# A recurrent attention block and a mixture of experts in one program: the low part of each split weight tile on GpSimd instead of VectorE

## Chip, cores and metric

The kernel runs on one core of a Trainium2 chip. The metric is the device time of one execution in microseconds; three runs of the kernel before gave 1008.19, 1009.38 and 1009.79 us, so the median is 1009.38 us. Engine names are those of the profile: PE is TensorE's matrix multiplication and PEld its weight load, DVE is VectorE, ACT is ScalarE, POOL is GpSimd, SP is SyncE, which here only issues DMAs.

## The reference

A gated linear attention, step by step in time, gives `x`; a mixture of four small two-layer networks is then applied to `x` and summed with normalised weights.

```python
for t in range(S):                      # B, H, S, D = 4, 8, 768, 48
    state = alpha[:, :, t, :, None] * state + einsum('bhd,bhe->bhde', k[:, :, t], v[:, :, t])
    y[:, :, t] = einsum('bhd,bhde->bhe', q[:, :, t], state)
x = y.transpose(0, 2, 1, 3).reshape(B * S, H * D)          # 3072 x 384
p = domain_probs / (domain_probs.sum(-1, keepdims=True) + 1e-09)
for e in range(E):                      # 4 experts, w1 384 x 1024, w2 1024 x 384
    out += p[:, e:e + 1] * (np.maximum(x @ w1[e], 0.0) @ w2[e])
```

## The kernel before

The sequence is cut into 24 units of 128 time steps (six chunks, four batches), and each unit's attention is a Python generator (`attention`, L422) that yields after every beat. Inside a unit a loop over seven levels doubles the block length. At each level ACT copies a part of the queries (L487), DVE multiplies the queries by decays (L494), shortens the decays (L496), ACT copies keys (L505), DVE multiplies the keys (L506), PE forms products (L513), and DVE puts them under a mask (L523). L539, L464 and L453 are other DVE multiplications, L434 the transposes that bring the inputs into place. So ACT and DVE take turns through a unit.

The units are gathered in groups: the first of two units, the others of four. For each group and expert, `up` (L660) multiplies by `w1` and `down` (L723) by `w2`. Group 0 works with plain fp32 weights and activations (L689, L764 with `raw`). From group 1 on both operands are split in two fp32r parts, a rounded top part and the remainder, and three products replace one (`PRODUCTS`, L95; L695 and L764 with `w`). The remainder of the hidden layer is made by L720 on DVE, for which PE can wait.

The weight tiles are split once, while group 0 and group 1 are computed. A piece is a quarter of one expert's `w1` or `w2`, 128 x 768 elements; there are 16 of each, 32 in all. `load_piece` (L178) brings the whole piece into a `raw` buffer (12 of them) by a DMA of SP. `split_piece` (L200) is a generator in two steps: the first takes a `w` buffer (four for each layer) and lets ACT write the rounded part `top` (L208); the second, one call of `background` (L213) later, subtracts it from the whole (L210) and stores both parts to HBM as one DMA of 768 KB from POOL's queue (L211). Later groups load both parts back from there (L185). In group 1 the pieces of `w2` are also used directly from the buffer in which they were made, by L764 in `down`.

The order of the instructions on each engine is the order in which the Python code calls them: the schedule is written out by hand. `background` is called after each step of `up`, and at some steps of `down`; `making` holds pieces not yet begun and `splitting` those with their second step to come. `advance` (L858) brings in the beats of attention by due times that the code computes from fixed costs. Each engine works through its own list in order, and waits on semaphores where it needs another's result.

Apart from the split, POOL has memsets in the first 10 us, and 22 stores of results (L799). For two of these units (the first group's) the store is issued between the stores of the 18th and 19th pieces.

Of the kernel before, what the change touches and what calls it, by code (L numbers as in the profile page):

```python
# [10 lines left out]
F32 = mybir.dt.float32  # L11
# [9 lines left out]
def kernel(  # L21
# [11 lines left out]
    nc = tc.nc  # L33
# [138 lines left out]
    def parts_of(l):  # L172
        return wts.tile([P, 2, KC * QF], F32R, name=f"w{l + 1}", bufs=AHEAD if l == 0 else NQ)
# [26 lines left out]
    def split_piece(l, i):  # L200
        gi, k = divmod(i, E * NQ)
        whole = wt[l][i]
        w = parts_of(l)
        if l == 1:
            wt[l][i] = w
        top, rest = (w[:, part] for part in range(2))

        nc.scalar.copy(out=top, in_=whole)  # L208
        yield
        nc.vector.tensor_sub(rest, whole, top.bitcast(F32))  # L210
        nc.gpsimd.dma_start(out=kept[l][k], in_=w.bitcast(F32))  # L211

    def background():  # L213
# [446 lines left out]
    def up(gi, e, fc, slots=None):  # L660
# [12 lines left out]
        if fresh(gi) and fc in beside:  # L673
            making.append(split_piece(1, first_piece(gi, e) + beside[fc]))
        if gi == 0 and e > 0 and fc in SPLIT_AT:
            making.append(split_piece(0, e * NQ + SPLIT_AT[fc]))
# [46 lines left out]
    def down(gi, e, slots):  # L723
# [4 lines left out]
        if gi == 0 and e < E - 1 and slots[0] == (e == 0):  # L728
            making.extend(split_piece(0, first + NQ + k) for k in range(2))
# [134 lines left out]
    with tc.manual_schedule():  # L864
# [46 lines left out]
        for gi, e in tasks:  # L911
            rest = gi == e == 0
# [37 lines left out]
```

## Time and profile before

| | |
|---|---|
| runs, us | 1008.19, 1009.38, 1009.79 |
| profiled execution, us | 1008.34 |
| its span, us | 1006.6 |
| granted TensorE clock, mean | 0.998 |
| L208, ACT, 128x768, 32 times | 26.4 us, 828 ns each, 37.5 to 288.7 us |
| L210, DVE, 128x768, 32 times | 30.3 us, 951 ns each, 38.8 to 293.9 us |
| L211, POOL, issue of a store, 32 times | 17.2 us, 537 ns each; 7.8 us to landing (median) |
| DVE, all | 569.3 us |
| POOL, all | 36.0 us |

The span is the time from the first to the last instruction of the program on the core; the device time has 1.7 us around it. Mean durations are of one instruction. The chain of waits is followed back from the last instruction, at each step to what released it or to the instruction in front of it on its engine; an instruction that isn't on it ended early enough. An engine's busy time includes time in which an instruction is held up after it has begun.

### The profile page before, as it was taken

The numbers are of one execution on the slowest core, as the hardware profiler recorded it, in microseconds if no ns is written. First come the engines' busy times: TensorE is split into PE (matmuls) and PEld (weight loads), VectorE is DVE, ScalarE is ACT, GpSimd is POOL, SyncE is SP. The second block draws the span as 40 slices with busy tenths as digits, with TensorE's granted clock in tenths as the row PEclk, the third lists the DMA queues.
The fourth block names the chain that finished last, engine by engine and source line by source line (L and its number), as shares of the span: only waits on it lengthen the run. The fifth ranks groups of instructions, "written<-read, shape, count | busy, mean of one in ns | idle before, by whom it ended". The sixth has DMA issues, their size and how long they took to land.

```text
span 1006.6 us, 20815 instructions
## 1 busy us (share of the span) xinstructions
PE 986.5 (98%) x8468; PEld 877.8 (87%) x8468; DVE 569.3 (57%) x1202; ACT 422.2 (42%) x928; POOL 36.0 (4%) x79
## 2 busy tenths in 40 slices
PE   8899899999999999999999999999999999999998
PEld 7767678988989889889899899898898989999998
DVE  5788878477666555566646635756576521222222
ACT  4677656454463542532543514445443422111111
POOL 2000001000000000000000000000000000000000
PEclk9999999999999999999999999999999999999999
DMA  9898989595776593764955928757757405151511
GB/s 190 264 295 214 308 267 346 165 336 142 284 256 203 195 272 96 263 216 136 312 166 160 305 99 236 246 134 277 225 156 251 158 2 202 49 210 41 199 68 32
DMA packets 160623, 200.81 MB, mean 199 GB/s; under 512 B 88432, under 2 KB 136944, under 8 KB 160528
## 3 DMA queue, kind: packets, MB, share of 16 engines
q1 hardware_dynamic: 154064, 169.66, 54.6%
q0 software_dynamic: 6016, 29.49, 7.5%
q8 instruction: 67, 1.10, 0.5%
q10 hardware_dynamic: 448, 0.33, 0.1%
q14 instruction: 28, 0.23, 0.1%
HBM read 169.56 MB, written 29.88 MB: 198 GB/s over the span
## 4 chain that ended last, share of the span: by engine, by line
PE 86%; DVE 7%; ACT 3%; issue 2%; DMA 1%; SPq 0%; DVEq 0%; POOL 0%; ACTq 0%; POOLq 0%
PE ops L764 38%; PE one L695 34%; PE sc L513 5%; PE yps L608 3%; ACT qb L487 1%; PE sps L639 1%; DVE w L210 1%; DVE near L523 1%; PE tp L236 1%; PE far L569 1%; PE one L689 1%; DVE QT L494 1%; DVE QT L434 1%; DVE hT L720 1%; DVE KT L506 1%
## 5 line engine op out<-in xcount | busy, mean ns | idle before, releaser
L764 PE MATMUL ops<-w,hT 128*128 128x384 f32 x2112 | 381.1, 338 | 0.6 <-DVE hT L720 0.6
L764 PEld LDWEIGHTS ops<-w,hT 128*128 128x128 f32 x2112 | 364.3, 188 | 5.2 <-DVE hT L720 1.8
L695 PE MATMUL one<-xT,w 128*128 128x512 f32 x1440 | 338.3, 393 | 0.0
L695 PEld LDWEIGHTS one<-xT,w 128*128 128x128 f32 x1440 | 268.8, 188 | 57.5 <-DVE hT L720 0.2
L697 ACT ACTIVATE hT<-one 128x512 fp32r<-128x512 f32 (+1 forms) x192 | 107.9, 562 | 295.3 <-PE one L695 294.3
L720 DVE SCALAR_TENSOR_TENSOR hT<-one,hT 128x512 fp32r<-128x512 f32 (+1 forms) x192 | 121.7, 642 | 116.0 <-ACT hT L697 116.0
L487 ACT COPY qb<-QT 64x256 f32<-64x256 f32 x322 | 131.3, 408 | 85.7 <-DVE QT L494 42.7
L494 DVE TENSOR_TENSOR QT<-QT,AT 128x256 f32<-128x256 f32 x158 | 66.7, 422 | 89.1 <-ACT qb L487 88.4
L790 DVE SCALAR_TENSOR_TENSOR acc<-ops,p_all,acc 128x384 f32<-128x384 f32 x66 | 38.2, 612 | 92.3 <-PE ops L764 92.2
L523 DVE COPY_PREDICATED near<-masks,sc 128x256 f32<-128x256 uint8 x138 | 73.9, 536 | 16.3 <-PE sc L513 13.7
L513 PEld LDWEIGHTS sc<-qb,KT 128*64 128x64 f32 x2208 | 69.8, 138 | 9.2 <-issue 4.4
L513 PE MATMUL sc<-qb,KT 128*64 128x64 f32 x2208 | 74.3, 223 | 3.1 <-ACT qb L487 3.0
L506 DVE TENSOR_TENSOR KT<-KT,AT 128x256 f32<-128x256 f32 x161 | 67.3, 418 | 0.8 <-PE tp L236 0.8
L505 ACT COPY KT<-KT 128x256 f32<-128x256 f32 x138 | 57.6, 418 | 3.3
L689 PE MATMUL one<-xT,raw 128*128 128x256 f32 (+1 forms) x240 | 45.1, 340 | 0.4 <-ACT xT L406 0.4
L764 PE MATMUL ops<-raw,hT 128*128 128x384 f32 x128 | 44.7, 492 | 0.0
L689 PEld LDWEIGHTS one<-xT,raw 128*128 128x128 f32 x240 | 38.1, 191 | 5.2 <-ACT xT L406 0.6
L445 ACT ACTIVATE AT<-AT,ident 128x512 f32<-128x512 f32 x22 | 15.9, 724 | 63.5 <-DVE AT L434 62.6
L496 DVE TENSOR_TENSOR AT<-AT 128x256 f32<-128x256 f32 (+1 forms) x138 | 39.2, 284 | 4.7
L799 POOL DMA_DIRECT2D out_dram<-acc x22 | 11.8, 540 | 680.2 <-DVE acc L790 680.2
L608 PE MATMUL yps<-lat,rv 128*32 128x128 f32 x736 | 33.1, 273 | 2.6 <-ACT lat L586 2.6
L764 PEld LDWEIGHTS ops<-raw,hT 128*128 128x128 f32 x128 | 23.2, 190 | 13.7 <-issue 0.6
(110 smaller groups left out, 638.5 us busy)
## 6 DMA issues: line engine op xcount, KB each, us to landing
w<-kept SPq DMA_DIRECT2D x144, 768.0 KB, 6.9
kept<-w POOLq DMA_DIRECT2D x32, 768.0 KB, 7.8
raw<-in_moe_w_dram SPq DMA_DIRECT2D x48, 384.0 KB, 7.5
rv<-in_v_dram SPq DMA_DIRECT2D x24, 192.0 KB, 2.9
rk<-in_k_dram SPq DMA_DIRECT2D x22, 192.0 KB, 3.6
rq<-in_q_dram SPq DMA_DIRECT2D x22, 192.0 KB, 7.8
out_dram<-acc POOLq DMA_DIRECT2D x22, 192.0 KB, 2.3
sa<-in_alpha_dram SPq DMA_DIRECT2D x44, 88.0 KB, 2.6
```

Source lines behind the costliest of these rows:

```text
L487: nc.scalar.copy(out=qb[rows, :, i, :].rearrange("p a (b r) -> p a b r", r=m), in_=qv[rows])
L494: nc.vector.tensor_mul(qv, qv, spread(dv[:, :, :, 0], m))
L505: nc.scalar.copy(out=new[:, :, :, 1, :], in_=old[:, :, :, 1, :])
L506: nc.vector.tensor_mul(new[:, :, :, 0, :], old[:, :, :, 0, :], spread(halved(decs[li])[:, :, :, 1], m))
L513: nc.tensor.matmul(out[HALF * s:HALF * (s + 1), 2 * p:2 * p + 2, :], lhsT=KTs[li][:, p, HALF * s:HALF * (s + 1)], rhs=qbs[li][:, p, :, QUA ...
L523: nc.vector.copy_predicated(near.rearrange("p a (b two r) -> p a b two r", two=2, r=m)[:, :, :, 1, :], mk.unsqueeze(1).broadcast_to([P, H, ...
L608: nc.tensor.matmul(yps[QUAD * j:QUAD * (j + 1), c, :], lhsT=lhsT, rhs=rhs, start=begins, stop=ends)
L689: nc.tensor.matmul(one, lhsT=w[:, kc], rhs=xTs[gi][:, 0, kc, lo:hi], start=(kc == 0), stop=(kc == KC - 1))
L695: nc.tensor.matmul(one, lhsT=w[:, of_w, kc], rhs=x_part(gi, of_x)[:, kc, :n], start=k == 0, stop=k == len(turns) - 1)
L697: nc.scalar.activation(out=parts[0], in_=one, func=ACT.Relu)
L720: nc.vector.scalar_tensor_tensor(out=low, in0=x, scalar=0.0, in1=top.bitcast(F32), op0=ALU.max, op1=ALU.subtract)
L764: nc.tensor.matmul(sums[slot], lhsT=h, rhs=w, start=(n == begins[slot]), stop=(n == ends[slot]))
```

## The change

```diff
         nc.scalar.copy(out=top, in_=whole)
         yield
-        nc.vector.tensor_sub(rest, whole, top.bitcast(F32))
+        nc.gpsimd.tensor_sub(rest, whole, top.bitcast(F32))
         nc.gpsimd.dma_start(out=kept[l][k], in_=w.bitcast(F32))
```

All 32 subtractions leave DVE's list and stand on POOL's list, each directly in front of its own store. The order of what is left on DVE, and of everything on PE, ACT and SP, stays as it was. In front of the first subtraction the build puts one instruction on POOL that fetches the code for it. The store waits for a semaphore of its own engine now, and POOL's subtraction carries the waits for `top`, for the loaded piece and for the buffer that DVE's carried.

## The prediction

> **What bounds the kernel now.** First the page's busy line and its slices, to see which engine sets the pace and where the work on the split lies.
>
> ```profile
> span 1006.6 us, 20815 instructions
> PE 986.5 (98%) x8468; PEld 877.8 (87%) x8468; DVE 569.3 (57%) x1202; ACT 422.2 (42%) x928; POOL 36.0 (4%) x79
> PE   8899899999999999999999999999999999999998
> DVE  5788878477666555566646635756576521222222
> ```
>
> A slice is 25.2 us. PE is at 9 nearly everywhere; below it are only the first two slices, the fifth and the last, and in the first six DVE is at 5 to 8. So I cut the span into stretches and read PE's busy time of each:
>
> ```profile
> 25.00:50.00 25.00, 21.87 (x249) 18.01 (x248) 18.15 (x41) 17.38 (x44) 2.27 (x4) 1.00 0.80 263
> 50.00:75.00 25.00, 23.18 (x182) 17.16 (x180) 21.74 (x44) 17.63 (x43) 2.12 (x4) 1.00 0.95 293
> 75.00:100.00 25.00, 23.13 (x282) 18.23 (x284) 20.75 (x46) 17.89 (x41) 1.60 (x3) 1.00 0.83 213
> 100.00:125.00 25.00, 21.95 (x246) 15.90 (x241) 22.48 (x49) 16.16 (x38) 1.59 (x3) 1.00 1.00 312
> 125.00:150.00 25.00, 23.71 (x188) 18.29 (x187) 17.67 (x40) 14.62 (x34) 1.06 (x2) 1.00 0.85 262
> ...
> 200.00:225.00 25.00, 24.43 (x186) 21.44 (x188) 18.87 (x35) 13.99 (x29) 2.13 (x4) 1.00 0.96 316
> ```
>
> The columns after the length are busy us of PE, PEld, DVE, ACT and POOL. From 25 to 150 us PE is idle for 3.13 + 1.82 + 1.87 + 3.05 + 1.29 = 11.2 us, and DVE is the fullest of the feeding engines (22.48 of 25). From 150 to 350 us PE lacks 0.7 us in all (0.57 of it in the line of 200 to 225). The change touches work between 37 and 295 us, so it can win only what PE stands idle up to 225, and above all before 150.
>
> Next the line that moves, and then the chain of waits (start, length, what):
>
> ```profile
> L210 DVE TENSOR_TENSOR w<-raw,w x32: 944/949/977, 38.8 to 293.9; 128x768 fp32r<-128x768 f32 x32
> ...
> 58.06 0.83 ACT w L208
> 58.92 0.96 DVE w L210
> 59.88 0.34 DVE QT L494
> ```
>
> L210 takes 0.95 us each time. Of the 32, 16 run before 150 us: four at 38 to 44, where DVE has gaps, and twelve from 57 to 137, where it has next to none. On the chain up to 150 us stand six of these (58.92, 62.13, 68.54, 83.02, 88.06, 132.21), together 5.67 us. After 150 seven more stand on it, but beside a PE that is full.
>
> **The change part by part.** Removed from DVE: 32 x 0.95 = 30.3 us. The four early ones run in gaps and are worth nothing. The last 16 are covered by PE's queue of L695 and L764; what they can give is the 0.57 us that PE waited at 214 us for L720. The twelve between are 12 x 0.95 = 11.4 us, with 5.67 on the chain: half. I use that share for DVE time that comes and goes in this stretch.
>
> Added to POOL: 32 subtractions of 128x768. No row has such an operation. The nearest are POOL's memsets, which only write.
>
> ```profile
> L873 POOL MEMSET rv<- 128x640 f32 x2 | 1.2, 629 | 0.1
> L875 POOL MEMSET st<- 128x384 f32 x3 | 1.2, 439 | 0.0
> ```
>
> They give 0.742 ns an element ((629 - 439)/256), so one pass over 768 is 629 + 128 x 0.742 = 724 ns, the lower bound. Two reads and a write, one after the other, add two passes of 570 ns: 1.86 us, the upper bound. I take 1.87 us, since the operation has three streams. The Trainium skill (GPSIMD Engine Reference, "Elementwise — side-by-side cycle accounting") gives 4497 ns for 2048 elements with two inputs, by proportion an estimate of 1.69 us; by it the sum below would be about 0.7 us better, and no run shown here has it.
>
> POOL's length is itself hidden. POOL is 4% busy, and per piece it now holds 1.87 us and the store's issue of 0.54 (L211). L208's end leads L210's start by up to 7 us (3 in the mean) because DVE is serving other work, so most subtractions end earlier than they do now, and with them the store, the load's reuse of `raw`, and PE's first use of `rest` in group 1 (down starts at 172.5 and 212.9 us; on POOL the four subtractions before them end near 164 and 210, now at 166 and 212). Behind a subtraction in POOL's queue stand only its own store, the next piece, and two L799 stores (0.54 each at 155.5 us, data ready), so nobody new waits for POOL. The first one also needs POOL's code for it, which the changed program fetches in an instruction of its own; POOL's 30 us of idle time before 40 us cover that. Without that cover it would delay the first store, which is not read back before 137.9 us.
>
> What remains is whether the two engines disturb each other while reading the same memory. No row shows POOL computing on inputs beside DVE. One end: not at all, nothing is lost. Other end: a DVE instruction with two inputs in SBUF (L494, L496, L506, L539, L464, L453) waits until POOL's subtraction is done. That I count on the timeline: POOL starts 0.08 us after L208 ends (my allowance; L210 follows it by 0.03 us where it had only that to wait for), holds 1.87 us, and the loss is what is left of it when the first such DVE instruction is due, L210 taken out. One example:
>
> ```profile
> 78.53 0.83 ACT L208 CAST w<-raw 128x768 fp32r<-128x768 f32 x1
> ...
> 79.77 0.56 DVE L621 TENSOR_TENSOR xT<-yps,xT 128x384 fp32r<-128x384 f32 x1 [1.32 <-ACT xT L620]
> 80.24 0.41 DVE L494 TENSOR_TENSOR QT<-QT,AT 128x256 f32<-128x256 f32 x1
> ```
>
> L208 ends at 79.36, POOL holds 79.44 to 81.31, L621 reads PSUM and passes, L494 is due at 80.25: 1.06 us lost. For the twelve pieces, in order: 1.2, 0, 1.15, 0.2, 1.05, 0 to 1.4, 0.5, 0, 0.45, 0.6 to 1.35, 1.2, 1.05: together 7.4 to 9.6 us, 0.6 to 0.8 each. I take this end rather than none, because instructions on two inputs fill about half of DVE's time here and POOL starts exactly where they come thickest; the other end is the first rival. The Trainium skill (SBUF — State Buffer, "Who interferes with whom") says that such a VectorE instruction and a GpSimd instruction that reads SBUF exclude each other for a whole instruction; no run shown here bears it out or refutes it, and it would leave the count as it stands.
>
> Sum: (11.4 - 8.5) x 0.5 = 1.4 us gained, between 0.9 and 2.0. Against the profiled run (1008.34 us, span 1006.6 and 1.7 around it): 1006.9. That run lies 1.0 us below the median shown, so on the median's scale 1009.4 - 1.4 = 1008.0.
>
> **The rivals.**
> *DVE is not held up at all.* For it: ACT reads SBUF beside DVE all the time, and L494 keeps 0.42 us. Against: L487 reads one tile, and no row has a second engine reading two. The 5.67 us leave the chain, but L487 on ACT, whose copies alternate with L494 level by level and stand on the chain with 8% from 25 to 165 us, takes over part: between half and all of 5.67, with 0.6 at 214 us at best. Middle 4.2: 1005.2; at best 1003.1.
> *The wait costs more than the instruction did* (the other side). Place: the level loop from 50 to 137 us, where L494 follows ACT's copies directly. ACT's next instruction after L208 is often the very copy that L494 waits for, and without L210 in front of it L494 is due earlier, just after POOL has begun. My count uses starts from a DVE that was not yet rearranged. It decides from 0.95 us of loss per piece on (11.4/12). With 1.5 us it is (18 - 11.4) x 0.5 = 3.3 us slower, 1012.7; with the full 1.87 each time (22.4 - 11.4) x 0.5 = 5.5, 1014.9. For it: up to seven of the twelve counted losses already lie at 1.05 or more. Against: the transposes L434 (1.1 us) and L523, which do not read two tiles of SBUF, give POOL cover.
> *Something else takes the wait.* The chain has DMA waits in the same stretch (2.38 us at 54.78 for `sq`, 2.01 at 95.97) that would just begin earlier: 1009.4.
>
> **How the numbers follow.** Under 0.2% (2 us) a measurement of this kernel can't tell from no change. My forecast has 0.38: split by its spread into faster 0.14, same 0.16, slower 0.08. No hold-up 0.20: faster 0.19, same 0.01. Costlier wait 0.35: slower 0.33, same 0.02. Other wait 0.07: same 0.05, 0.01 to each side. Sum: faster 0.34, same 0.24, slower 0.42. The forecast's own range is 1006.5 to 1009.5; with the rivals' ends it is 1003.2 to 1015.0.
>
> **What would show it.** Right: 32 POOL tensor operations of about 1.9 us; L494, L496, L506 or L464 lengthened (or started late) by 0.5 to 1.9 us beside them and of the old length elsewhere; DVE's busy sum in 50 to 150 us little changed; PE's idle time before 150 us near 10 us; from 150 us on everything shifted by one amount. Wrong: those DVE lines at their old 0.42 us beside POOL (first rival), PE idle over 13 us before 150 (second), new waits of PE for `w` from POOL, or of ACT's L208 for a late store, or a POOL operation beyond 2 us.

## The result, and the profile after

The changed kernel takes 1013.78 us (median of six runs, 1013.24 to 1014.93) beside 1009.09 us of the kernel before: a ratio of 1.0046, 95% interval 1.0030 to 1.0061. It is slower by 4.7 us, where the forecast had it 1.4 us faster. The profiled execution has 1014.51 us and a span of 1012.3, 5.7 more than before. First the page's busy line:

```profile
span 1012.3 us, 20818 instructions
PE 987.2 (98%) x8468; PEld 877.6 (87%) x8468; DVE 566.6 (56%) x1170; ACT 422.5 (42%) x928; POOL 96.5 (10%) x111
```

32 instructions have left DVE, each of 0.95 us, 30.3 us in all. But DVE's busy time fell only from 569.3 to 566.6 us. Nearly all of the other 27.6 us must be in instructions that were there before (about three of them are L210's overlap with its neighbours). The groups by line show which, first of the kernel before, then of the changed one:

```profile
L506 DVE TENSOR_TENSOR KT<-KT,AT 128x256 f32<-128x256 f32 x161 | 67.3, 418 | 0.8 <-PE tp L236 0.8
L494 DVE TENSOR_TENSOR QT<-QT,AT 128x256 f32<-128x256 f32 x158 | 66.7, 422 | 89.1 <-ACT qb L487 88.4
...
L453 DVE TENSOR_TENSOR rk<-rq,rk 128x384 f32<-128x384 f32 x22 | 12.0, 545 | 0.0
```

```profile
L494 DVE TENSOR_TENSOR QT<-QT,AT 128x256 f32<-128x256 f32 x158 | 78.4, 496 | 92.8 <-ACT qb L487 91.9
L523 DVE COPY_PREDICATED near<-masks,sc 128x256 f32<-128x256 uint8 x138 | 74.0, 537 | 16.2 <-PE sc L513 13.7
L506 DVE TENSOR_TENSOR KT<-KT,AT 128x256 f32<-128x256 f32 x161 | 72.5, 450 | 0.9 <-PE tp L236 0.9
...
L453 DVE TENSOR_TENSOR rk<-rq,rk 128x384 f32<-128x384 f32 x22 | 16.1, 733 | 0.6 <-DMA rq<-in_q_dram 0.6
```

L494 went from a mean of 422 to 496 ns, L506 from 418 to 450, L453 from 545 to 733. L523, which reads a mask and PSUM, stayed (536, now 537). The timeline shows single ones; first DVE, then POOL, in the place that the prediction worked through:

```profile
80.44 0.56 DVE L621 TENSOR_TENSOR xT<-yps,xT 128x384 fp32r<-128x384 f32 x1 [1.31 <-ACT xT L620]
80.91 1.33 DVE L494 TENSOR_TENSOR QT<-QT,AT 128x256 f32<-128x256 f32 x1
...
82.40 2.56 DVE L506 TENSOR_TENSOR KT<-KT,AT 128x256 f32<-128x256 f32 x1
...
80.12 1.84 POOL L210 TENSOR_TENSOR w<-raw,w 128x768 fp32r<-128x768 f32 x1 [10.11 <-ACT w L208]
82.26 0.57 POOL L211 DMA_DIRECT2D kept<-w  x1 [0.30 <-DMA sq<-in_q_dram]
82.85 1.82 POOL L210 TENSOR_TENSOR w<-raw,w 128x768 fp32r<-128x768 f32 x1
```

L621 (one operand in PSUM) runs its usual 0.56 us beside POOL. L494, usually 0.42, stays until 82.24, just past the end of POOL's subtraction at 81.96. L506 stays from 82.40 to 84.96, past the end of the next one at 84.67. Over the span 20 instructions are lengthened, all of L494, L506, L453, L539 and L464, by 24.3 us together and by at most 2.13 us.

The stretches show what it cost (busy us of PE, PEld, DVE, ACT, POOL after the length):

```profile
25.00:50.00 25.00, 21.85 (x249) 18.01 (x248) 16.10 (x37) 17.47 (x44) 9.72 (x8) 1.00 0.76 235
50.00:75.00 25.00, 22.90 (x182) 17.38 (x180) 20.80 (x39) 16.89 (x42) 9.64 (x8) 1.00 0.99 316
75.00:100.00 25.00, 21.36 (x214) 16.22 (x216) 21.09 (x40) 16.59 (x37) 7.22 (x6) 1.00 0.85 225
100.00:125.00 25.00, 21.94 (x288) 16.23 (x284) 20.20 (x46) 17.73 (x42) 7.34 (x6) 1.00 1.01 310
125.00:150.00 25.00, 23.56 (x217) 18.53 (x208) 16.88 (x35) 13.94 (x32) 4.79 (x4) 1.00 0.74 233
150.00:175.00 25.00, 24.27 (x167) 18.46 (x167) 20.05 (x33) 13.51 (x27) 10.83 (x10) 1.00 1.06 350
...
200.00:225.00 25.00, 23.92 (x149) 20.49 (x148) 19.11 (x32) 16.67 (x34) 9.72 (x8) 1.00 0.83 253
...
250.00:275.00 25.00, 24.20 (x259) 21.70 (x259) 19.11 (x37) 13.00 (x29) 5.44 (x5) 1.00 1.02 344
```

PE idles 13.4 us from 25 to 150 us (before: 11.2), and it now idles in three stretches after that, 2.6 us in these lines, where it had been full but for 0.6. Laid beside those of before, DVE's instructions run 2.4 us late at 147 us and 5.5 us late from 304 us on. So the loss comes in both stretches, and ends where the last subtraction ends (297 us).

Before 150 us the hold reaches PE by way of ACT. PE's products of line 569 wait for a copy of ACT. From 50 to 150 us these waits (total, times, longest) were, in the kernel before:

```profile
PE far L569 <- ACT qb L487: 2.2, 2, 1.3
```

and in the changed one:

```profile
PE far L569 <- ACT qb L487: 5.1, 3, 1.9
```

DVE is held, ACT's copy L487 starts late, and PE waits for that copy. All of PE's waits there together grow from 7.9 to 10.2 us.

### The profile page after: what moved, and what is told of

It reads as the page before. It is cut to its first block, busy times and chain, and to the rows that moved or that the text cites. A ratio compares the mean times of both kernels' runs of the same rounds, so it can differ in the third digit from the quotient of the medians.

```text
span 1012.3 us, 20818 instructions
## 1 busy us (share of the span) xinstructions
PE 987.2 (98%) x8468; PEld 877.6 (87%) x8468; DVE 566.6 (56%) x1170; ACT 422.5 (42%) x928; POOL 96.5 (10%) x111
## 4 chain that ended last, share of the span: by engine, by line
PE 81%; DVE 8%; DMA 4%; ACT 4%; issue 2%; SPq 1%; POOL 0%; DVEq 0%; ACTq 0%
PE ops L764 37%; PE one L695 31%; PE sc L513 5%; PE yps L608 3%; ACT qb L487 2%; DMA rq<-in_q_dram 1%; DVE QT L494 1%; DVE near L523 1%; PE sps L639 1%; PE tp L236 1%; PE one L689 1%; PE far L569 1%; DMA w<-kept 1%; DMA raw<-in_moe_w_dram 1%; DVE hT L720 1%
## 5 line engine op out<-in xcount | busy, mean ns | idle before, releaser
L695 PE MATMUL one<-xT,w 128*128 128x512 f32 x1440 | 339.5, 393 | 2.2 <-DVE hT L720 2.1
L695 PEld LDWEIGHTS one<-xT,w 128*128 128x128 f32 x1440 | 268.5, 188 | 61.4 <-DVE hT L720 4.5
L720 DVE SCALAR_TENSOR_TENSOR hT<-one,hT 128x512 fp32r<-128x512 f32 (+1 forms) x192 | 121.4, 642 | 116.2 <-ACT hT L697 116.0
L487 ACT COPY qb<-QT 64x256 f32<-64x256 f32 x322 | 131.4, 408 | 90.2 <-DVE QT L494 45.0
L494 DVE TENSOR_TENSOR QT<-QT,AT 128x256 f32<-128x256 f32 x158 | 78.4, 496 | 92.8 <-ACT qb L487 91.9
L523 DVE COPY_PREDICATED near<-masks,sc 128x256 f32<-128x256 uint8 x138 | 74.0, 537 | 16.2 <-PE sc L513 13.7
L210 POOL TENSOR_TENSOR w<-raw,w 128x768 fp32r<-128x768 f32 x32 | 59.2, 1851 | 199.8 <-ACT w L208 199.4
L506 DVE TENSOR_TENSOR KT<-KT,AT 128x256 f32<-128x256 f32 x161 | 72.5, 450 | 0.9 <-PE tp L236 0.9
L496 DVE TENSOR_TENSOR AT<-AT 128x256 f32<-128x256 f32 (+1 forms) x138 | 39.2, 284 | 4.7
```

What stands on the lines that cost most here:

```text
L210: nc.gpsimd.tensor_sub(rest, whole, top.bitcast(F32))
L487: nc.scalar.copy(out=qb[rows, :, i, :].rearrange("p a (b r) -> p a b r", r=m), in_=qv[rows])
L494: nc.vector.tensor_mul(qv, qv, spread(dv[:, :, :, 0], m))
L506: nc.vector.tensor_mul(new[:, :, :, 0, :], old[:, :, :, 0, :], spread(halved(decs[li])[:, :, :, 1], m))
L523: nc.vector.copy_predicated(near.rearrange("p a (b two r) -> p a b two r", two=2, r=m)[:, :, :, 1, :], mk.unsqueeze(1).broadcast_to([P, H, ...
L695: nc.tensor.matmul(one, lhsT=w[:, of_w, kc], rhs=x_part(gi, of_x)[:, kc, :n], start=k == 0, stop=k == len(turns) - 1)
```

## The experiments

All ratios are to runs of the kernel before that were made beside them on the same chip. The first four were to tell what holds DVE, and where it costs.

**POOL writes, but does not read.**

```diff
-        nc.vector.tensor_sub(rest, whole, top.bitcast(F32))
+        for n in (KC * QF, KC * QF, KC * QF // 2):
+            nc.gpsimd.memset(rest.bitcast(F32)[:, :n], 0.0)
```

> The subtraction on POOL is replaced by three memsets into the same `rest` (768, 768 and 384 columns), about 0.73 + 0.73 + 0.44 = 1.9 us of POOL time by the memset rows, with the same store behind them. The remainders of the weights are left out of the result. DVE is free of L210 as in the changed kernel, and POOL is as busy, but reads nothing. Theory A (DVE's instructions with two SBUF inputs are held while POOL reads SBUF): no DVE instruction is lengthened, L494 back at 0.42 us in the mean, and the time falls below the kernel before, to 1004 to 1008 us, since L210 is gone for nothing. Rival B (POOL's later end, its queue or its code, and the later store, cost the time): 1012 to 1014 us, as the changed kernel.

1005.49 us, ratio 0.9962 (0.9950 to 0.9974). The groups by line, where the added line makes L494 into L495:

```profile
L507 DVE TENSOR_TENSOR KT<-KT,AT 128x256 f32<-128x256 f32 x161 | 67.3, 418 | 1.7 <-PE tp L237 1.7
L495 DVE TENSOR_TENSOR QT<-QT,AT 128x256 f32<-128x256 f32 x158 | 67.0, 424 | 100.0 <-ACT qb L488 99.1
...
L211 POOL MEMSET w<- 128x768 f32 x64 | 47.8, 748 | 76.8 <-PE ops L765 72.7 <-DVE w L312 2.3
```

POOL has as much to do as in the changed kernel (1.9 us and a store for each piece), 58 two-input instructions of DVE run beside its memsets, and not one is lengthened by more than 0.1 us. So a busy POOL is not the cause; that it reads is. Two differences remain: the memsets need not wait for `top`, so they start at other moments, and the stores behind them are issued sooner. The fetch of code, which this kernel does not need, is cleared by the trace of the changed kernel: it shows as two instructions (MODIFY_POOL_CONFIG) of 17 ns at 9.7 us, and the first subtraction starts at 38.46 us, 0.1 us after its L208 has ended. The kernel also measures the gain that the change aimed at: 3.8 us.

**One half at a time.**

```diff
-        nc.vector.tensor_sub(rest, whole, top.bitcast(F32))
+        (nc.gpsimd if l == 0 else nc.vector).tensor_sub(rest, whole, top.bitcast(F32))
```

> Only the 16 pieces of w1 (38 to 138 us) are subtracted on POOL, the 16 of w2 stay on DVE. Theory A by the lag of DVE's instructions between the two traces (2.4 us up to 147 us, 5.5 at the end): 1009.1 + 2.4 = 1011.5 us. Rival C (what is lost is lost before 150 us alone, because PE covers the rest, as the prediction had it): all of it, 1013.8 us.

and the same with `l == 1`:

> Only the 16 pieces of w2 (151 to 296 us) are subtracted on POOL, the 16 of w1 stay on DVE. Theory A: DVE held as in the changed kernel, L720 late, PE waits for it: 1009.1 + 3.1 = 1012.2 us. Rival C (PE's queue covers this stretch): 1009 us, as before, or up to 0.6 below.

1011.38 us, ratio 1.0019 (1.0010 to 1.0027), and 1012.04 us, ratio 1.0029 (1.0020 to 1.0038). With the ratios it is 1.9 and 2.9 us, 4.8 together, what the whole change costs. Rival C falls: PE's queue does not cover the second stretch. Who waits for whom on PE between 150 and 305 us (total, times, longest), second half on POOL:

```profile
PE one L695 <- DVE hT L720: 1.5, 3, 0.7
PE ops L764 <- DVE hT L720: 0.4, 1, 0.4
```

L720 reads PSUM and is not held itself, but stands behind L453, L464 or L494 that are. Before, PE waited for it once, for 0.57 us. These waits account for 1.3 us of the 2.9; where the rest arises was not found.

**POOL reads one stream.**

```diff
-        nc.vector.tensor_sub(rest, whole, top.bitcast(F32))
+        for _ in range(2):
+            nc.gpsimd.tensor_copy(out=rest, in_=whole)
```

> The subtraction on POOL is replaced by two copies of the whole piece into `rest`, so POOL reads one stream instead of two; by the memset rows some 1.5 to 1.9 us for both. The remainders are wrong by this, so their part of the result is left out. Theory A in its wide form (any reading by POOL holds DVE's two-input instructions): L494 lengthened up to the end of a copy, by at most about 0.9 us each, and 1010 to 1013 us. In its narrow form (only a POOL instruction with two inputs holds them): L494 at 0.42 us and 1004 to 1008 us.

1011.29 us, ratio 1.0021 (1.0005 to 1.0037). A copy takes 889 ns; 27 instructions of DVE are lengthened by 0.1 us or more, by 14.8 us together and by 1.02 us at most; ten of them are L496, which the changed kernel never has beside POOL. DVE and POOL in the place looked at above (one added line makes L494 into L495 and L496 into L497):

```profile
79.69 1.31 DVE L495 TENSOR_TENSOR QT<-QT,AT 128x256 f32<-128x256 f32 x1
81.03 0.72 DVE L497 TENSOR_TENSOR AT<-AT 128x32 f32<-128x32 f32 x1
...
79.87 1.81 POOL L211 CAST w<-raw 128x768 fp32r<-128x768 f32 x2
```

The wide form holds: one stream that POOL reads is enough, and here a hold is not longer than about one copy. The lengthened instructions show this, and the time less so: the granted clock of these runs was 0.995 in the mean, beside 0.997 before, and the profiled execution, at 0.997, took 1009.27 us, no more than the kernel before.

**The subtraction in six slices.**

```diff
-        nc.vector.tensor_sub(rest, whole, top.bitcast(F32))
+        for s in range(0, KC * QF, P):
+            nc.gpsimd.tensor_sub(rest[:, s:s + P], whole[:, s:s + P], top.bitcast(F32)[:, s:s + P])
```

> The subtraction on POOL is cut into six of 128 columns. POOL's time for a piece grows, by some 0.1 us of start for each slice, to 2.3 us or more. Theory A1 (DVE is held by one POOL instruction as a whole, and comes in between two): no DVE instruction is lengthened by more than one slice, about 0.4 us, instead of up to 2.1; many more are lengthened, and the time falls to 1009 to 1012 us. Theory A2 (POOL keeps DVE out as long as its queue holds instructions that read, as the holds that begin before POOL's recorded start may mean): lengthened by 2 us and more as in the changed kernel, 1013 to 1016 us.

1011.44 us, ratio 1.0017 (1.0008 to 1.0026), although a slice takes 509 ns where a sixth of a whole one is 309, so that POOL reads for much longer. 48 instructions are lengthened by 0.1 us or more instead of 20, by 18.1 us together instead of 24.3, and 44 of them by 0.1 to 0.3: DVE does come in between two POOL instructions. But not always: four are lengthened by 1.8 to 2.7 us. DVE and POOL in one such place (this kernel's L507 is L506):

```profile
213.45 3.08 DVE L507 TENSOR_TENSOR KT<-KT,AT 128x256 f32<-128x256 f32 x1
...
213.67 2.56 POOL L211 TENSOR_TENSOR w<-raw,w 128x128 fp32r<-128x128 f32 x6
```

An instruction that DVE began 0.2 us before the first slice waited for all six. Neither theory is right alone. What decides whether DVE gets in between is open.

**What L210 alone is worth in the first stretch.**

```diff
-        nc.vector.tensor_sub(rest, whole, top.bitcast(F32))
+        if l == 0:
+            for n in (KC * QF, KC * QF, KC * QF // 2):
+                nc.gpsimd.memset(rest.bitcast(F32)[:, :n], 0.0)
+        else:
+            nc.vector.tensor_sub(rest, whole, top.bitcast(F32))
```

> The 16 pieces of w1 get the three memsets on POOL in place of the subtraction (their remainders are left out of the result), the 16 of w2 are subtracted on DVE as before. It measures what L210 alone is worth in the first stretch. The chain of waits before (5.67 us on it, 11.2 us of idle PE before 150 us) and the full PE after it say that nearly all of the 3.8 us that both halves together gave comes from here: 1005.5 to 1006.5 us. Rival (the removal in the second stretch is worth as much as the holds there cost): 1007 to 1008 us.

1005.79 us, ratio 0.9963 (0.9951 to 0.9975), the same as with both halves. The gain of 3.7 us is all in the first stretch, and taking L210 from DVE in the second is worth nothing measurable. So, by difference, the holds alone cost 1.9 + 3.7 = 5.6 us in the first stretch (give or take 1.5, by the intervals) and 2.9 in the second. The mean granted clock of the runs was 0.997 here, with POOL that only writes, and before, so the clock does not explain the gain.

**Only pieces that had no harmful hold.**

```diff
-        nc.vector.tensor_sub(rest, whole, top.bitcast(F32))
+        no_loss = (0, 1, 2, 3, 5, 7, 11, 12, 18, 23, 26, 30)
+        engine = nc.gpsimd if E * NQ * l + k in no_loss else nc.vector
+        engine.tensor_sub(rest, whole, top.bitcast(F32))
```

> Only the pieces behind which the trace of the changed kernel shows no hold that moved anything (the 1st to 4th, 6th, 8th, 12th, 13th, 19th, 24th, 27th and 31st) are subtracted on POOL, the others on DVE. Theory A: if holds are all that costs, and the stretch keeps its rhythm, most of the gain of the removed L210 of the four between 57 and 117 us stays without the holds: 1006 to 1008.5 us, faster than the kernel before. Rival (the rhythm shifts and new holds come): 1009 to 1011 us.

1012.44 us, ratio 1.0023 (1.0013 to 1.0032): slower. The rhythm shifted. It has six holds, 7.9 us together; only the first, in a gap at 39 us, was there in the changed kernel. Three of the five new ones are on L464 (1.46 to 2.22 us instead of 0.69). A place free of holds in one trace is not free in the next kernel.

**POOL under cover that the program sets.** The subtraction is handed on to the places in `attention` where DVE reads one input for a while, and a pair of tiny memsets keeps POOL from starting sooner.

```diff
-        nc.vector.tensor_sub(rest, whole, top.bitcast(F32))
-        nc.gpsimd.dma_start(out=kept[l][k], in_=w.bitcast(F32))
+        def rest_and_store(engine):
+            engine.tensor_sub(rest, whole, top.bitcast(F32))
+            nc.gpsimd.dma_start(out=kept[l][k], in_=w.bitcast(F32))
+        if l == 1:
+            rest_and_store(nc.vector)
+        elif k < NQ:
+            rest_and_store(nc.gpsimd)
+        else:
+            if len(held_back) == 2:
+                held_back.popleft()(nc.vector)
+            held_back.append(rest_and_store)
...
+    def under_cover():
+        if held_back:
+            nc.vector.memset(mark, 0.0)
+            nc.gpsimd.memset(mark, 0.0)
+            held_back.popleft()(nc.gpsimd)
```

`under_cover` is called ahead of `turn("a", AT)` and of `reduce_sum`, from unit 2 on. What is still held back when `load_piece` first reads a stored piece is done on DVE there.

> A version that tries to keep the gain. The first four pieces of w1 go to POOL as in the changed kernel; of the next twelve, up to two are held back until a unit of attention begins, and are subtracted on POOL from there, one beside the transposes of a and k (L434, 2.1 us) and one beside the sum L454 and the transpose of q (1.65 us), where DVE reads one input only. A one-column memset on DVE and one on POOL behind it set the start. Seven pieces go that way, five stay on DVE, and all of w2's. Theory A: the seven hold DVE for at most some 0.3 us each, and the gain is about 7/12 of the 3.7 us that the first stretch gives, less the marks: 1007 to 1008.3 us beside 1009.5 before. Rival (starts slip past the cover, or the later places and stores cost more): 1009 to 1011 us, with holds of over 1 us on L453 or L464.

> The control of it: the same pieces held back to the same places, but all subtracted on DVE, without marks. DVE's time is that of the kernel before. If the places alone do nothing: 1008.5 to 1010.5 us. If they are worth or cost something by themselves it shows here.

1012.18 us, ratio 1.0027 (1.0015 to 1.0039), and the control on DVE 1016.04 us, ratio 1.0066 (1.0053 to 1.0078). Both are slower than before, so the new places cost by themselves. At the same places POOL is 3.9 us better than DVE (the control also has the first four pieces on DVE). In the covered kernel PE idles 10.3 us from 25 to 150 us (before 11.2), but then waits 2.5 us at once, until 171.4 us, for L720. That L720 stood behind L453, for which DVE waited 2.61 us until a load of queries (`rq`) had landed. From 171 to 174 us, right behind the wait, the granted clock reads 0.51, and nine L695 took 3.75 us instead of 2.08. The pieces held back last, the suspects, went back to their old place:

```diff
-        if l == 1:
+        if l == 1 or k >= 3 * NQ:
             rest_and_store(nc.vector)
```

> As the covered version, but the last four pieces of w1 stay where they were, on DVE, so that neither their buffers nor the loads of w2 behind them come late; held back are only the 5th to 12th. If lateness at 150 us was what the covered version lost, PE's 2.5 us wait there goes, and it is about 2.5 us faster than that one: 1008.5 to 1010 us, near the kernel before. If the places of the held-back pieces cost by themselves: 1011 to 1013 us.

1008.19 us, ratio 0.9981 (0.9971 to 0.9991): faster than the kernel before by 1.9 us. By the ratios the last four pieces had cost the covered version 4.6 us. The wait and the stretch of low clock behind it, both gone here, are 2.5 + 1.7 = 4.2 us in the profiled executions. In the covered version the loads of w2's pieces, which stand ahead of that `rq` in SP's list, were issued from 145.28 us on instead of 142.53 (here 143.27); that this is what made `rq` late fits the order, but was not tried by itself. Four pieces of the group run in DVE's gaps and six under cover; five instructions are lengthened, 3.8 us together, 1.6 of it in the gap. Some of the stretches:

```profile
50.00:75.00 25.00, 23.66 (x199) 17.88 (x201) 20.52 (x45) 18.87 (x46) 5.50 (x7) 1.00 0.94 290
75.00:100.00 25.00, 23.59 (x293) 18.49 (x285) 19.72 (x44) 18.57 (x43) 5.18 (x7) 1.00 0.88 232
...
150.00:175.00 25.00, 25.00 (x196) 20.04 (x195) 20.59 (x41) 14.76 (x31) 3.21 (x6) 1.00 1.07 349
```

PE has 23.66 and 23.59 us where it had 23.18 and 23.13, and is full again from 150 us. From 25 to 150 us it idles 9.1 us, before 11.2. The profiled execution is not itself a faster one (1009.08 us beside 1008.34): PE idles 5.3 us in its first 25 us, before 3.6, ahead of the first subtraction. So the gain rests on the twelve runs beside the twenty-two before. How much of it comes from the six pieces under cover and how much from the four in gaps was not separated, and there is no control on DVE for this version. A last one held back only one piece at a time, with the longer cover (the same edit with `len(held_back) == 1`, and without the call ahead of `reduce_sum`):

> As the one beside it, but only one piece is held back at a time and goes to POOL beside the transposes of a and k, the longest cover; the place at L454 is not used. Fewer pieces leave DVE, and fewer holds of L464 come: 1008 to 1010 us if cover decides, 1011 or more if the places cost.

1008.58 us, ratio 0.9992 (0.9981 to 1.0003): no difference that can be told from the kernel before. It has only two holds over 0.2 us, but only seven pieces on POOL.

## Why the prediction was wrong

*POOL's price* came out right, 1.87 us assumed and 1.851 measured, but by luck. It was worked out as three passes over the data, one after the other, each as long as the next but for a fixed part. In the experiments a memset of 768 columns takes 748 ns, a copy of them 889 and the subtraction 1851: the first stream that is read adds 0.14 us, the second 0.96. The proportion from the Trainium skill's figure (GPSIMD Engine Reference, "Elementwise — side-by-side cycle accounting") gave 1.69, too little.

*That DVE is held* was right, and so was the count for the twelve pieces: 7.4 to 9.6 us were counted, and 9.9 us are lost before 150 us, 1.6 of them by the first piece, which ran in a gap as foreseen; 8.3 remain. In part the sum agrees because errors cancel: two losses are longer than POOL's whole subtraction (1.93 and 2.14 us, counted 1.15 and 0 to 1.4), since DVE was held from before POOL's recorded start, and eight are smaller than counted. The kernel that only writes confirms the reason. The Trainium skill (SBUF — State Buffer, "Who interferes with whom") says the same: a two-input VectorE instruction contends with a GpSimd instruction that reads SBUF, not with one that only writes it. All three parts agree with runs here: writing 0 of 58 lengthened, reading one stream 27, two streams 20.

*The failing step is the share of one half*, which the prediction used for DVE time that goes and for DVE time that comes. Measured, 11.4 us of L210 taken away gave 3.7 us, a share of 0.33; 8.3 us of holds cost 5.6 us, a share of 0.67. By the intervals of the runs the first lies between 0.2 and 0.4, the second between 0.5 and 0.9. With 0.33 and 0.67 the sum (11.4 x 0.33 - 8.3 x 0.67) is -1.8 us, a loss; the shares come from these runs, so they must give about what the first half alone measured (1.9), but with one common share for both no loss could come out, since 8.3 is less than 11.4. The reason shows at 62 us. DVE and ACT of the kernel before:

```profile
62.13 0.98 DVE L210 TENSOR_TENSOR w<-raw,w 128x768 fp32r<-128x768 f32 x1
63.03 0.40 DVE L494 TENSOR_TENSOR QT<-QT,AT 128x256 f32<-128x256 f32 x1
...
63.46 0.82 ACT L487 COPY qb<-QT 64x256 f32<-64x256 f32 x2 [1.24 <-DVE QT L494]
```

DVE, POOL and ACT of the changed kernel:

```profile
62.58 2.35 DVE L494 TENSOR_TENSOR QT<-QT,AT 128x256 f32<-128x256 f32 x1 [1.06 <-ACT qb L487]
...
62.81 1.83 POOL L210 TENSOR_TENSOR w<-raw,w 128x768 fp32r<-128x768 f32 x1
...
64.96 0.82 ACT L487 COPY qb<-QT 64x256 f32<-64x256 f32 x2 [1.70 <-DVE QT L494]
```

In the changed kernel DVE had been idle for 1.06 us, waiting for ACT: there the DVE time that L210 gave back lay unused. The hold then fell on L494 itself, whose result ACT waits for, and ACT stood 1.70 us, where it had stood 1.24 behind L210. ACT's copies L487 show what each was worth. Four in a row begin at 55.44, 56.74, 60.71 and 63.46 us before, and at 55.49, 57.84, 61.73 and 64.96 after. The hold of L494 at 56.35 (1.03 us) makes ACT 1.05 us later. The two L210 that are gone at 57.87 (2.00 us) win back 0.08. The hold at 62.58 (1.93 us, where an L210 of 0.98 stood) costs another 0.48. In such a place L210 was something that could be done while the two wait for each other; a hold falls on an instruction in their exchange. That the whole difference of the shares comes from this was not counted place by place.

*The cover after 150 us* was the second failing step. The prediction let PE's queue cover the last 16 pieces for the gain, and booked nothing for a loss. For the gain that was right (nothing measurable). For the holds it was not: with only the second half on POOL, 12.2 us of them cost 2.9 us. At least 1.3 of it comes about because L720 stands behind the held instruction and PE waits for L720. So the sign that everything would be shifted by one amount from 150 us on failed: the lag grows from 2.4 to 5.5 us.

*The rivals.* "Not held up at all" had a middle of 4.2 us; without holds it is 3.7 to 3.8, but that needs a POOL that does not read. "The wait costs more than the instruction did" has the right side, its sign (PE idle over 13 us before 150, measured 13.4) and nearly the time (1012.7), but not its point of decision: it was to turn at 0.95 us of loss for a piece, and the mean was 8.3/12 = 0.69. It too put all the loss before 150 us, so that its time comes near the measured one is luck. The sign of the change turned on which instruction the lost time falls on. The prediction's chances had slower as the likeliest (0.42); its single forecast, faster, came from the common share.

## What to carry to other kernels

A cheap engine that reads the same memory is not free: price the move by what it holds up on the other engine, and weigh a hold by the instruction that it falls on, not by the mean share of that engine on the chain. Saved time and lost time of an engine have different prices, and a queue that covers a saving need not cover a loss. Picking places that were quiet in an earlier trace did not work. Letting the program itself start the move under cover gave one version that was faster, by 1.9 us, of three: the first was slower, the last the same.

## What the runs showed of the hardware

A DVE instruction can be held by a POOL instruction that starts after it in the trace: L464 began at 253.17 us, 0.4 us before POOL's subtraction at 253.57, and lasted 2.82 us instead of 0.69. The Trainium skill (SBUF — State Buffer, "SBUF: two separate sides") says that whichever of such a VectorE instruction and a GpSimd instruction starts first has the shared ports for the whole instruction. By the recorded starts that is not so here, in this place and in at least four others (L494 at 62.58 and 206.49, L506 at 82.40, and L506 at 213.45 in the sliced kernel). In all of them POOL's reading instruction came directly behind its own DMA issue. Four other instructions of the changed kernel also began before POOL's recorded start, by 0.2 to 0.7 us (L464 at 94.14, L539 at 102.04, L453 at 112.82, L506 at 117.75), and kept their length; there POOL had been idle for 2.0 to 9.3 us. The DMA issue alone does not hold DVE: in the kernel before, 38 such instructions run beside an issue of L211, and none is lengthened. Whether POOL claims the memory before its recorded start, when its next instruction is already waiting, was not tried.
